# VectorE instead of GpSimd for the low halves of the output weights in the first token block of the first expert layer

## The chip, the cores and the metric

The kernel runs on one core of a Trainium2 chip. The metric is the device time of one execution in microseconds (us), as the median of several executions. One execution was recorded with the hardware profiler; its trace gives every instruction's start and duration. The engines are called as in the profile: PE is TensorE's matrix multiplication and PEld its weight load, DVE is VectorE, ACT is ScalarE, POOL is GpSimd, SP is the engine that issues most of the DMAs.

## The reference, cut to what matters

Three stages follow each other: an attention over 4 x 448 tokens whose heads are mixed before and after the softmax, a dense layer ("first expert layer" here) and a layer of eight experts. The change lies in the dense layer alone, for 1792 tokens:

```python
def _moe_ref(x, w_in, w_out):          # x 1792 x 768
    h = x @ w_in                       # 768 -> 2048
    g = h - np.tanh(h)
    return (g @ w_out).astype(np.float32)   # 2048 -> 768
```

## The kernel before

The dense layer is the function moe1. It cuts the tokens into four blocks of 512, 512, 512 and 256, and the 2048 inner columns into 16 parts of 128; a unit (b, f) is part f of block b. For each unit `first(b, f)` makes the 128 x 512 product h on PE (18 matmuls, line 541), in one of two PSUM banks that alternate (`bank(6)`), and the nonlinearity from it: ACT writes u, d and the two squares (lines 547 to 550), VectorE combines them into g by six instructions (lines 551 to 556), ACT rounds g to ghl's high half (line 558), GpSimd subtracts that from g to get its low half (line 559). Two units later `second(b, f)` multiplies (18 matmuls, line 569): for each of six output chunks high x high, high x low half of g, low half of the weight x high.

The weight halves are whl. `split_wo(b, f)` makes them anew for every block out of wo[f], one unit ahead: ACT rounds to the high half (line 489), and another engine subtracts for the low half, the "rest" (line 490, 128 x 768). In blocks 0 to 2 that engine is GpSimd, in the last block VectorE. whl and ghl have three buffers each.

In block 0 alone, wo[f] itself is made first. `load_wo(f)` loads 64-bit numbers into wor (768 KB, one buffer, line 483), and three VectorE instructions (lines 77, 79 and 81) turn them into float32. As there is one wor, the load of part f+1 starts when line 81 of part f is over. In block 0 VectorE also prepares tables for the routing of the last layer: small instructions on es (8 x 1, lines 436 to 446 and 524), em (line 525), tri (520) and en (532). The router's table en passes through one of the two banks after unit 6 (`prepare_turn`), so that unit 7 gets the bank of unit 6 again, and its first matmul waits until VectorE's line 552 of unit 6 has read it.

Every engine works through its own list in order; the lists are set when the program is built, by a scheduler that works with estimates of durations, so an edit of one instruction can reorder its neighbours.

Of the kernel before, what the change touches and what calls it, by code (L numbers as in the profile page):

```python
# [11 lines left out]
F32 = mybir.dt.float32  # L12
# [28 lines left out]
BLOCKS = [(0, 512), (512, 512), (1024, 512), (1536, 256)]  # L41
# [407 lines left out]
def moe1(tc, ctx, bank, xd, wind, w_out, emb, tau, consts, yg, pos, keep, ids0, chosen):  # L449

    nc = tc.nc
# [13 lines left out]
    wih, wil, wo = {}, {}, {}  # L465
# [21 lines left out]
    def split_wo(b, f):  # L487
        w = p3.tile([128, 2, DM], F32R, tag="whl", name=f"whl_{b}_{f}")
        nc.scalar.copy(w[:, 0], wo[f])  # L489
        (nc.vector if b == len(BLOCKS) - 1 else nc.gpsimd).tensor_tensor(out=w[:, 1], in0=wo[f], in1=w[:, 0].bitcast(F32),  # L490
                                                                         op=ALU.subtract)
        W[b, f] = w

# [272 lines left out]

    units = [(b, f) for b in range(len(BLOCKS)) for f in range(FC)]
    split_wo(0, 0)
    todo = []
    for i, (b, f) in enumerate(units):  # L770
# [6 lines left out]
        if i + 1 < len(units):  # L777
            split_wo(*units[i + 1])
# [386 lines left out]
```

## Time and profile before

| | us |
|---|---|
| time before, median of 3 executions | 1247.13 (1244.72 to 1248.77) |
| profiled execution | 1242.88 |
| its span, first to last instruction | 1241.0 |
| PE busy in the span | 1181.6 (95%) |
| VectorE, ScalarE, GpSimd busy | 852.2, 730.7, 628.2 |
| line 490 on GpSimd, blocks 0 to 2 (48 times) | 89.4, 1863 ns each |

Attention ends at about 462 us; block 0 of the dense layer then fills the time to about 610 us, blocks 1 to 3 that to 949 us, and the expert layer the rest. In the rows below, "idle before" is an engine's idle time just ahead of an instruction, with what ended it behind the arrow. Names without numbers stand for all their buffers.

### The profile page before, as it was taken

How to read it: one execution, taken by the hardware profiler on the slowest of the kernel's cores; microseconds unless marked ns; L12 is line 12 of the kernel's file. 1: busy time of each engine (PE TensorE's matmuls, PEld its weight loads, DVE VectorE, ACT ScalarE, POOL GpSimd, SP SyncE). 2: the span in 40 equal slices, each digit the busy share in tenths (PEclk: the TensorE clock that was granted, in tenths of full speed). 3: DMA queues.
4: the chain of work that ended last, by engine and by line, in shares of the span. 5: the costliest groups of instructions: out<-in, count | busy, mean ns of one | idle time of the engine just before them, and what ended most of it. 6: DMA issues, size and time to landing. Idle time of an engine off the chain costs nothing.

```text
span 1241.0 us, 23758 instructions
## 1 busy us (share of the span) xinstructions
PE 1181.6 (95%) x8624; PEld 834.3 (67%) x8648; DVE 852.2 (69%) x1943; ACT 730.7 (59%) x1499; POOL 628.2 (51%) x546
## 2 busy tenths in 40 slices
PE   8999999999999988999999999999998899999994
PEld 4655665665566654566566666666887678899993
DVE  5887687778877829977767447654788455566661
ACT  6887687678768744444545454554577234555661
POOL 3887688578858753433453335243233233343340
PEclk8999998999999999999999999999999899999998
DMA  6465656556565486223201000010034656678750
GB/s 199 161 215 154 203 186 207 154 190 197 177 197 193 128 246 218 79 100 107 73 1 52 1 26 2 1 51 1 1 130 154 196 192 200 213 253 278 247 201 23
DMA packets 82872, 173.92 MB, mean 140 GB/s; under 512 B 12171, under 2 KB 60171, under 8 KB 82744
## 3 DMA queue, kind: packets, MB, share of 16 engines
q1 hardware_dynamic: 77002, 160.75, 39.9%
q0 software_dynamic: 5472, 11.43, 3.4%
q8 instruction: 70, 1.15, 0.4%
q14 instruction: 58, 0.48, 0.1%
q10 hardware_dynamic: 270, 0.12, 0.1%
HBM read 110.79 MB, written 23.30 MB: 108 GB/s over the span
## 4 chain that ended last, share of the span: by engine, by line
PE 68%; DVE 11%; DMA 9%; issue 4%; ACT 4%; POOL 3%; SPq 1%; ACTq 0%; POOLq 0%; DVEq 0%
PE bank L569 11%; PE bank L541 10%; PE bank L290 9%; PE bank L240 9%; PE bank L948 9%; PE bank L924 9%; PE bank L203 4%; PE bank L305 4%; DMA G<-S 3%; DMA wor<-in_w_out_dram 3%; DVE g L555 1%; DVE wo L81 1%; DVE wo L79 1%; PE bank L977 1%; DVE g L556 1%
## 5 line engine op out<-in xcount | busy, mean ns | idle before, releaser
L569 PE MATMUL bank<-ghl,whl 128*128 128x512 f32 (+1 forms) x1152 | 257.3, 374 | 8.4 <-POOL whl L490 3.0
L569 PEld LDWEIGHTS bank<-ghl,whl 128*128 128x128 f32 x1152 | 198.2, 190 | 49.6 <-POOL whl L490 4.7
L295 POOL TENSOR_TENSOR at<-at 128x480 f16<-128x480 f32 x180 | 176.2, 990 | 48.7 <-ACT at L294 45.7
L240 PE MATMUL bank<-G,wmix 120*120 120x448 f32 x360 | 171.9, 562 | 9.8 <-DMA G<-S 9.0
L290 PE MATMUL bank<-wr,A 120*128 120x120 f32 (+4 forms) x1800 | 171.0, 243 | 3.9 <-DVE wr L272 3.1
L490 POOL TENSOR_TENSOR whl<-wo,whl 128x768 fp32r<-128x768 f32 x48 | 89.4, 1863 | 160.3 <-ACT whl L489 159.8
L244 DVE TENSOR_REDUCE st<-bank 120x1 f32<-120x448 f32 x180 | 111.6, 620 | 52.8 <-PE bank L240 50.5
L250 ACT ACTIVATE A<-bank,st 120x448 f32<-120x448 f32 x180 | 114.9, 639 | 47.4 <-DVE st L244 24.4
L559 POOL TENSOR_TENSOR ghl<-g,ghl 128x512 fp32r<-128x512 f32 (+1 forms) x64 | 78.2, 1221 | 127.3 <-ACT ghl L558 127.3
L294 ACT COPY at<-bank 128x480 f32<-128x480 f32 x180 | 101.6, 566 | 33.1 <-PE bank L290 32.8
L541 PEld LDWEIGHTS <-wih 128*128 128x128 f16 x768 | 71.6, 98 | 72.3 <-issue 13.4
L913 ACT CAST wh_a<-wr_a 128x768 f16<-128x768 f32 x112 | 92.6, 829 | 43.0 <-PE bank L948 33.6
L290 PEld LDWEIGHTS bank<-wr,A 120*128 120x128 f32 (+1 forms) x720 | 91.4, 193 | 36.1 <-issue 20.2
L551 DVE SCALAR_TENSOR_TENSOR g<-bank,u 128x512 f32<-128x512 f32 (+1 forms) x64 | 39.9, 623 | 97.6 <-ACT d L548 97.6
L914 DVE TENSOR_TENSOR wl_a<-wr_a,wh_a 128x768 bf16<-128x768 f32 x84 | 82.4, 983 | 33.6 <-ACT wh_a L913 33.5
L255 POOL TENSOR_TENSOR A<-A 120x448 f16<-120x448 f32 (+1 forms) x90 | 84.4, 938 | 28.2 <-ACT A L250 14.3
L489 ACT CAST whl<-wo 128x768 fp32r<-128x768 f32 x64 | 53.2, 833 | 76.5 <-PE bank L569 56.6
L948 PE MATMUL bank<-rh_a,wl_a 128*128 128x208 f16 (+5 forms) x336 | 86.2, 260 | 0.0
L948 PE MATMUL bank<-rl_a,wh_a 128*128 128x208 bf16 (+5 forms) x336 | 86.2, 260 | 0.0
L924 PE MATMUL bank<-xph_a,wh_a 128*128 128x208 f16 (+5 forms) x336 | 86.2, 259 | 0.0
L948 PE MATMUL bank<-rh_a,wh_a 128*128 128x208 f16 (+5 forms) x336 | 86.2, 259 | 0.0
L541 PE MATMUL bank<-mxh,wih 128*128 128x512 f16 (+1 forms) x384 | 84.1, 354 | 2.1 <-DVE d L552 2.0
(215 smaller groups left out, 2593.1 us busy)
## 6 DMA issues: line engine op xcount, KB each, us to landing
wr_a<-in_w_dram SPq DMA_DIRECT2D x64, 768.0 KB
G<-S SPq DMA_DIRECT2D x176, 210.0 KB
raw_w<-in_w_in_dram SPq DMA_DIRECT2D x32, 384.0 KB
wor<-in_w_out_dram SPq DMA_DIRECT2D x16, 768.0 KB
raw_v<-in_v_dram SPq DMA_DIRECT2D x16, 384.0 KB
yg<-row SPq DMA_DIRECT2D x3, 1540.0 KB
raw_q<-in_q_dram SPq DMA_DIRECT2D x9, 448.0 KB
raw_k<-in_k_dram SPq DMA_DIRECT2D x9, 448.0 KB
```

Of the source, the lines that this page charges most:

```text
L240: nc.tensor.matmul(ps[:r, :S], wmix[:r, :r], g[:r], start=True, stop=True)
L244: latest["dve"] = nc.vector.tensor_reduce(out=st[:r, k:k + 1], in_=ps[:r, :S], axis=AX.X, op=ALU.min)
L250: latest["act"] = nc.scalar.activation(out=a[:r, :S], in_=ps[:r, :S], func=AF.Exp, bias=bias, scale=-1.0, accum_out=st[:r, 4 + k:5 + k])
L290: nc.tensor.matmul(ps[:, jc * r:jc * r + r], x[:r, js], w[:r].rearrange("p (a b) -> p a b", b=10)[:, :, :n], start=(i == 0), stop=(i == le ...
L294: nc.scalar.copy(at32[:, :, t0:t0 + n], v)
L295: nc.gpsimd.tensor_tensor(out=atl[:, :, t0:t0 + n], in0=at32[:, :, t0:t0 + n], in1=ath[:, :, t0:t0 + n], op=ALU.subtract)
L490: (nc.vector if b == len(BLOCKS) - 1 else nc.gpsimd).tensor_tensor(out=w[:, 1], in0=wo[f], in1=w[:, 0].bitcast(F32), op=ALU.subtract)
L541: nc.tensor.matmul(h, u[f][:, c], X[b][v][:, c, :N], start=(i == 0), stop=(i == len(seq) - 1))
L569: nc.tensor.matmul(Y[b][c][:, :N], w[:, u, 128 * c:128 * c + 128], hl[:, v, :N], start=(f == 0 and i == 0), stop=(f == FC - 1 and i == 2))
L913: nc.scalar.copy(wh, raw)
L924: nc.tensor.matmul(h, w[u][:, 128 * c:128 * c + 128], XP[e][v][:, c, :N], start=(i == 0), stop=(i == len(seq) - 1))
L948: nc.tensor.matmul(O[e][c][:, :N], w[u][:, 128 * c:128 * c + 128], r[v], start=(f == 0 and i == 0), stop=(f == MF - 1 and i == 2))
```

## The change

In block 0 too, line 490 is given to VectorE.

```diff
     def split_wo(b, f):
         w = p3.tile([128, 2, DM], F32R, tag="whl", name=f"whl_{b}_{f}")
         nc.scalar.copy(w[:, 0], wo[f])
-        (nc.vector if b == len(BLOCKS) - 1 else nc.gpsimd).tensor_tensor(out=w[:, 1], in0=wo[f], in1=w[:, 0].bitcast(F32),
+        (nc.vector if b in (0, len(BLOCKS) - 1) else nc.gpsimd).tensor_tensor(out=w[:, 1], in0=wo[f], in1=w[:, 0].bitcast(F32),
                                                                          op=ALU.subtract)
```

This takes 16 instructions off GpSimd's list and puts them on VectorE's, and the scheduler places them. The first place is VectorE's list around unit 3, part 2 (in names the first number is the block or wo's part, and g_0_3 is unit 3 of block 0). Before:

```order
L551 SCALAR_TENSOR_TENSOR g_0_3_6737<-bank6_607_6716,u_0_3_6735 128x512
L79 SCALAR_TENSOR_TENSOR wo_2_6581<-wor_2_6579,wo_2_6581 128x768
L552 SCALAR_TENSOR_TENSOR d_0_3_6736<-bank6_607_6716,d_0_3_6736 128x512
L81 SCALAR_TENSOR_TENSOR wo_2_6581<-wor_2_6579,wo_2_6581 128x768
L553 TENSOR_SCALAR u_0_3_6735<-u_0_3_6735 128x512
L554 SCALAR_TENSOR_TENSOR g_0_3_6737<-s1_0_3_6738,g_0_3_6737 128x512
L443 TENSOR_SCALAR es_6514<-es_6514 8x1
L555 SCALAR_TENSOR_TENSOR g_0_3_6737<-s2_0_3_6739,g_0_3_6737 128x512
```

The same place of the changed kernel:

```order
L551 SCALAR_TENSOR_TENSOR g_0_3_6737<-bank6_607_6716,u_0_3_6735 128x512
L79 SCALAR_TENSOR_TENSOR wo_2_6581<-wor_2_6579,wo_2_6581 128x768
L552 SCALAR_TENSOR_TENSOR d_0_3_6736<-bank6_607_6716,d_0_3_6736 128x512
L81 SCALAR_TENSOR_TENSOR wo_2_6581<-wor_2_6579,wo_2_6581 128x768
L553 TENSOR_SCALAR u_0_3_6735<-u_0_3_6735 128x512
L554 SCALAR_TENSOR_TENSOR g_0_3_6737<-s1_0_3_6738,g_0_3_6737 128x512
L438 TENSOR_SCALAR es_6514<-es_6514 8x1
L490 TENSOR_TENSOR whl_0_2_6585<-wo_2_6581,whl_0_2_6585 128x768
L555 SCALAR_TENSOR_TENSOR g_0_3_6737<-s2_0_3_6739,g_0_3_6737 128x512
```

Line 490 has gone in among the steps of g, and the small es instructions lie one group later. For whl_0 to whl_5 it stands so, among the steps of g; whl_5's stands behind line 552 of unit 6. From whl_6 on it stands at another place, directly behind line 81 and ahead of line 551 of the next unit. This is VectorE's list there, unit 9, as a difference:

```order
 L556 COPY_PREDICATED g_8_7112<-u_8_7110,d_8_7111 128x512
 L81 SCALAR_TENSOR_TENSOR wo_7016<-wor_7014,wo_7016 128x768
+L490 TENSOR_TENSOR whl_8_7020<-wo_7016,whl_8_7020 128x768
 L551 SCALAR_TENSOR_TENSOR g_9_7180<-bank_614_7159,u_9_7178 128x512
 L552 SCALAR_TENSOR_TENSOR d_9_7179<-bank_614_7159,d_9_7179 128x512
```

Nothing else moved there. PE, ACT and SP keep their lists but for one neighbour exchanged on PE at unit 3 and one on ACT.

## Rows read from the trace of the kernel before

**Rows 1.** Busy time by stretch (windows): length, each engine's busy us, granted clock, DMA.

```profile
470.00:526.00 56.00, 48.84 (x205) 28.50 (x207) 54.06 (x77) 22.56 (x38) 22.88 (x13) 0.97 0.44 150
526.00:606.00 80.00, 79.74 (x356) 50.55 (x360) 58.27 (x85) 36.95 (x60) 34.18 (x21) 1.00 0.32 109
622.00:948.00 326.00, 321.19 (x1837) 229.12 (x1851) 211.27 (x441) 181.29 (x331) 124.36 (x92) 1.00 0.11 39
```

**Rows 2.** Waits of PE from 470 to 530 us: total, times, longest.

```profile
PE bank L569 <- POOL whl L490: 3.0, 3, 1.2
PE bank L541 <- DVE d L552: 2.0, 1, 2.0
```

**Rows 3.** Timeline about unit 7's start: start, duration, engine, line, instruction.

```profile
517.85 0.67 DVE L552 SCALAR_TENSOR_TENSOR d<-bank,d 128x512 f32<-128x512 f32 x1
...
518.57 1.72 PE L541 MATMUL bank<-mxh,wih 128*128 128x512 f16 x6 [1.98 <-DVE d L552]
...
523.95 4.48 PE L569 MATMUL bank<-ghl,whl 128*128 128x512 f32 x18
```

**Rows 4.** Windows of PE alone there: length, busy, granted clock, DMA.

```profile
518.00:520.00 2.00, 1.43 (x6) 0.91 0.78 200
520.00:522.00 2.00, 1.78 (x5) 0.50 0.47 194
```

**Rows 5.** VectorE from 478 to 518 us, grouped by line: busy us, mean ns.

```profile
L555 DVE SCALAR_TENSOR_TENSOR g<-s,g 128x512 f32<-128x512 f32 x4 | 9.1, 2277 | 0.1
```

**Rows 6.** VectorE from 526 to 598 us, grouped by line.

```profile
L555 DVE SCALAR_TENSOR_TENSOR g<-s,g 128x512 f32<-128x512 f32 x9 | 6.2, 686 | 0.1
```

**Rows 7.** Timeline of units 1 to 5, waits of VectorE and GpSimd on each other.

```profile
477.02 0.56 DVE L77 TENSOR_SCALAR wo<-wor 128x768 uint32<-128x768 uint32 x1 [0.43 <-DMA wor<-in_w_out_dram]
...
479.00 1.28 POOL L559 TENSOR_TENSOR ghl<-g,ghl 128x512 fp32r<-128x512 f32 x1 [3.09 <-ACT ghl L558]
...
479.61 1.48 DVE L81 SCALAR_TENSOR_TENSOR wo<-wor,wo 128x768 uint32<-128x768 uint32 x1
...
482.04 2.27 POOL L490 TENSOR_TENSOR whl<-wo,whl 128x768 fp32r<-128x768 f32 x1 [1.76 <-ACT whl L489]
...
482.66 2.20 DVE L555 SCALAR_TENSOR_TENSOR g<-s,g 128x512 f32<-128x512 f32 x1
...
486.43 1.25 DVE L442 TENSOR_TENSOR es<-es 8x1 f32<-8x1 f32 x1
...
505.35 0.56 DVE L77 TENSOR_SCALAR wo<-wor 128x768 uint32<-128x768 uint32 x1 [0.36 <-DMA wor<-in_w_out_dram]
...
505.94 1.94 DVE L79 SCALAR_TENSOR_TENSOR wo<-wor,wo 128x768 uint32<-128x768 uint32 x1
...
515.38 1.94 DVE L81 SCALAR_TENSOR_TENSOR wo<-wor,wo 128x768 uint32<-128x768 uint32 x1
```

**Rows 8.** Line 490's own instructions: ns shortest, median, longest, first and last start.

```profile
L490 DVE TENSOR_TENSOR whl<-wo,whl x16: 947/958/959, 861.3 to 936.1; 128x768 fp32r<-128x768 f32 x16
```

**Rows 9.** Timeline of one later unit.

```profile
548.01 4.46 PE L569 MATMUL bank<-ghl,whl 128*128 128x512 f32 x18
...
549.12 0.96 DVE L81 SCALAR_TENSOR_TENSOR wo<-wor,wo 128x768 uint32<-128x768 uint32 x1
...
550.04 1.29 POOL L559 TENSOR_TENSOR ghl<-g,ghl 128x512 fp32r<-128x512 f32 x1 [4.84 <-ACT ghl L558]
550.18 0.84 ACT L489 CAST whl<-wo 128x768 fp32r<-128x768 f32 x1 [0.21 <-DVE wo L81]
...
552.10 0.69 DVE L551 SCALAR_TENSOR_TENSOR g<-bank,u 128x512 f32<-128x512 f32 x1 [2.01 <-ACT d L548]
...
554.51 0.56 DVE L77 TENSOR_SCALAR wo<-wor 128x768 uint32<-128x768 uint32 x1 [0.19 <-DMA wor<-in_w_out_dram]
...
556.02 4.46 PE L569 MATMUL bank<-ghl,whl 128*128 128x512 f32 x18
...
557.10 0.95 DVE L81 SCALAR_TENSOR_TENSOR wo<-wor,wo 128x768 uint32<-128x768 uint32 x1
```

## The prediction

> **What bounds the kernel now.** I read the busy time by stretch first. Block 0 falls into two parts. From 526 us on PE is busy for 79.74 of 80 us, and in blocks 1 to 3 for 321.19 of 326; nothing that VectorE or GpSimd does shortens those, unless it makes PE wait. From 470 to 526 us PE is busy for 48.84 of 56 us only, and VectorE for 54.06: here VectorE is the full engine, and the 7.2 us in which PE idles are nearly all that the change can win [rows 1]. The waits of PE in that stretch name two things that touch the change: 3.0 us for line 490 on GpSimd, and one wait of 2.0 us for line 552 on VectorE [rows 2]. The timeline shows the second: line 552 of unit 6 ends at 518.52 us, and only then can unit 7's first matmul start, after 1.98 us of idleness, in the one bank that two units in a row share [rows 3]. From there PE runs without a gap. So the end of block 0, and with it the end of the kernel, moves one for one with the moment at which VectorE is through line 552 of unit 6. What PE waits for before that moment only makes it wait longer there: removing the 3.0 us alone buys nothing. That idle time also costs clock: the granted clock is 0.91 and then 0.50 (the lower of the two levels, 1.2 GHz) in the two windows behind it [rows 4], and unit 7's 18 matmuls take from 518.57 to 523.95 us [rows 3], 5.4 us, where a whole later unit of 36 takes 8.01 us, of which the second 18 take 4.46 [rows 9]: some 1.8 us lost.
>
> **The change, part by part.** The sum is made on VectorE's list, from line 81 of part 1, which ends at 481.09 us [rows 7], to line 552 of unit 6, which ends at 518.52.
>
> First, what is removed. GpSimd's line 490 runs while VectorE stands at line 555. In the first case GpSimd's instruction ends at 482.04 + 2.27 = 484.31 us, and line 555, begun at 482.66, ends at 484.86, 0.55 us later [rows 7]: it did its work once GpSimd was through. Line 555 has two inputs in SBUF, one of them g, the other a square from ACT. From 478 to 518 us the four of line 555 take 2277 ns each [rows 5], the nine later ones 686 ns [rows 6]: 4 x 1.59 = 6.4 us come back when GpSimd has no line 490.
>
> The Trainium skill says the same of the cause (SBUF — State Buffer, "Who interferes with whom"): a VectorE instruction with two SBUF inputs and a GpSimd instruction that reads SBUF exclude each other, and whichever was first holds the port for its whole length. The trace agrees (0.55 us after 484.31).
>
> Second, what is added. Between the two points VectorE gets whl_1 to whl_4; whl_0 comes before, whl_5 behind line 552 of unit 6. The trace has line 490 on VectorE in the last block, same shape, 958 ns [rows 8]: 4 x 0.96 = 3.8 us. whl_0 costs nothing: VectorE then waits for the load of part 1 until 477.02 us (0.43 us idle) [rows 7]; without that cover it would be 0.96.
>
> Third, GpSimd's line 559 (1.28 us) stays, and holds VectorE in the same way: line 81 at 479.61 us takes 1.48 instead of 0.95 us [rows 7, 9]. In the stretch of the sum it costs VectorE now at most 1.25 us at 486.43, and 0.99 us each at 505.94 and 515.38 (1.94 against 0.95): 3.2 us [rows 7]. In the new order lines 77 and 79 of the next part stand right behind line 556 in every unit, and line 559 starts about when line 79 wants the port, so I take four full waits: 4 x 0.99 = 4.0, that is 0.8 us more. Bounds: none more; or five waits, 1.8 us more.
>
> Fourth, the start and the load. In the new order line 81 of part 1 stands ahead of line 551 of unit 2 and behind line 556 of unit 1, so it ends before line 559 gets going, and the stretch begins 0.5 us earlier (its 1.48 us becomes 0.95). The load of a part starts when line 81 of the part before ends; line 77 waited 0.36 us for one at 505.35 [rows 7]. VectorE arrives sooner for parts 4 and 5, so I take 0.2 us more of that, with bounds of 0 and 0.4.
>
> Sum: 6.4 - 3.8 - 0.8 + 0.5 - 0.2 = 2.1 us less. Best by the bounds: 6.4 - 3.8 + 0.5 = 3.1 less. Worst: five line 490 (4.8), 1.8, 0.4 and no earlier start: 6.4 - 7.0 = 0.6 us more.
>
> Fifth, the later units (whl_6 to whl_15). VectorE has room, 58.27 us busy of 80 [rows 1], but its chain is tight: line 81 recurs after 7.98 us (549.12 to 557.10), PE's line 569 after 8.01 [rows 9]. Line 490 stands ahead of line 551 of the next unit, which idles 2.01 us for ACT. Line 81 ends at 550.08; ACT's cast ends at 551.02; GpSimd's line 559 holds the port to 551.33; line 490, if held till then, ends at about 552.2, where line 551 began at 552.10 [rows 9]. So it is hidden in that idle time but for 0.1 us, and that by the 0.19 us for which line 77 waited for its load anyway. I take nothing. Without this cover each unit's chain would grow by 0.96 - 0.19 = 0.77 us. Blocks 1 to 3 and GpSimd's remaining work are untouched.
>
> The profiled execution took 1242.88 us, so 1240.8 for such a one. It is 1.8 us below the fastest of the three executions timed; their median is 1247.13, and the same 2.1 us off it gives 1245.0.
>
> **The rivals.** (a) The clock stays up: if PE's wait before unit 7 gets short, the 1.8 us go too, 3.9 us in all, 1243.2. For it: VectorE is earlier by 2.1 us, more than the wait of 1.98. Against: PE comes earlier too, since the 3.0 us for line 490 fall away, so the wait rather grows, to about 1.98 + 3.0 - 2.1 = 2.9 us, and then the low clock stays.
>
> (b) Slower: VectorE, full as it is, just gets longer. If the waits of line 555 were not GpSimd's line 490 but would come at another instruction of the same stretch, nothing of the 6.4 us comes back: 3.8 + 0.8 + 0.2 - 0.5 = 4.3 us more, 1251.4. It decides from the point at which less than 4.3 / 4 = 1.1 of the 1.59 us per unit returns. For it: 54.06 of 56 us, and line 559 that is free to move into every gap. Against: the 0.55 us above.
>
> The Trainium skill speaks for this side (Perfetto Trace Analysis, "Optimizing Scalar/DVE Operations"): work that is moved between GpSimd and VectorE might not gain, as they share a read port. By that alone the time would not fall. The trace bears the sharing out, but the same subtraction takes 2.27 us on GpSimd there, its own waiting included [rows 7], and 0.96 on VectorE [rows 8].
>
> (c) The later chain: line 490 fails to fit into the idle time, and VectorE's chain grows by 0.77 us in each of ten units, 7.7 us. PE would feel only what goes beyond its lead: ghl is finished at 551.33 us for a line 569 at 556.02, 4.7 us [rows 9]. So 3.0 us come through, and with the 2.1 won it is 0.9 more, 1248.0. Against: the sums above, which leave 0.1 us.
>
> **How the numbers follow.** 0.3% is 3.7 us, about what a measurement can tell from no change. The forecast, with its own range from 3.1 less to 0.6 more (1244.0 to 1247.7), has a chance of 0.58 and lies within 0.3%. (a) has 0.20 and is just faster; (b) 0.10 and slower; (c) 0.12 and the same. So faster 0.20, the same 0.70, slower 0.10. The executions before spread from 1.6 above to 2.4 below their median, so the range goes from (a) less 2.4 to (c) plus 1.6: 1240.8 to 1249.6. It leaves out (b) and the far edges of the others.
>
> **What would show it.** Right: line 555 from 478 to 518 us at about 0.69 us; line 490 on VectorE at 0.96 us, with or without a wait for line 559; no wait of PE for line 490 on GpSimd; line 552 of unit 6 about 2 us earlier and PE's wait for it 2 to 3 us; line 569 still every 8.01 us later on. Wrong: the clock at full level behind unit 7's start (a); waits of VectorE behind line 559 that add up to more than 6 us (b); line 569 at more than 8.1 us in the later units (c).

## The result, and the profile after

The changed kernel took 1234.30 us as the median of 6 executions (1233.18 to 1238.42), against 1247.34 of 6 of the kernel before: 0.9913 of the time, with a 95% interval of 0.989 to 0.9935. The forecast was 1245.0 and its range ended at 1240.8. Two more sets of executions gave 0.9929 (0.9905 to 0.9952) and 0.994 (0.9917 to 0.9963), so the first set lay at the low end. Over all sets, 25 executions of after have a mean span of 1235.7 us and 134 of before one of 1244.1: 8.4 us less, four times the 2.1 that were forecast. The profiled execution of after took 1235.33 us with a span of 1233.6. One execution of a later experiment, late_units, took 1976 us at a granted clock of 0.556, and is left out of all means.

Busy time by stretch, after (length; busy us of PE, PEld, DVE, ACT, POOL; granted clock; DMA):

```profile
470.00:526.00 56.00, 51.47 (x228) 31.39 (x227) 51.06 (x88) 23.48 (x38) 9.71 (x7) 1.00 0.42 146
526.00:606.00 80.00, 79.64 (x371) 49.84 (x373) 66.53 (x96) 39.10 (x65) 17.32 (x12) 1.00 0.30 99
```

VectorE's busy time fell from 54.06 to 51.06 us in the first stretch although it has more instructions [rows 1]: what it lost is time spent holding still. VectorE grouped by line from 478 to 518 us (busy, mean ns | idle before), after:

```profile
L79 DVE SCALAR_TENSOR_TENSOR wo<-wor,wo 128x768 uint32<-128x768 uint32 x5 | 7.7, 1536 | 0.1
...
L490 DVE TENSOR_TENSOR whl<-wo,whl 128x768 fp32r<-128x768 f32 x5 | 4.7, 948 | 0.0
L555 DVE SCALAR_TENSOR_TENSOR g<-s,g 128x512 f32<-128x512 f32 x5 | 3.4, 689 | 0.1
```

Line 555 went from 2277 to 689 ns [rows 5], line 490 costs 948 ns, and line 79 now waits behind line 559. The stretch of the sum ends at 512.91 us, so one of the five of lines 79, 490 and 555 lies behind it. One small es instruction waits behind line 559 too, after:

```profile
490.93 1.29 POOL L559 TENSOR_TENSOR ghl<-g,ghl 128x512 fp32r<-128x512 f32 x1 [6.32 <-ACT ghl L558]
491.11 1.12 DVE L444 TENSOR_TENSOR es<-es 8x1 f32<-8x1 f32 x1
```

PE's waits from 470 to 530 us, after:

```profile
PE bank L541 <- DVE d L552: 3.4, 2, 3.2
PE bank L569 <- POOL ghl L559: 0.7, 1, 0.7
PE bank L569 <- DVE whl L490: 0.3, 1, 0.3
```

The 3.0 us of waits for GpSimd's line 490 are gone and the wait for line 552 has grown from 2.0 to 3.2 us [rows 2]. The timeline there, after:

```profile
508.78 1.93 DVE L79 SCALAR_TENSOR_TENSOR wo<-wor,wo 128x768 uint32<-128x768 uint32 x1
...
512.23 0.68 DVE L552 SCALAR_TENSOR_TENSOR d<-bank,d 128x512 f32<-128x512 f32 x1
512.96 1.46 PE L541 MATMUL bank<-mxh,wih 128*128 128x512 f16 x6 [3.16 <-DVE d L552]
...
516.65 4.46 PE L569 MATMUL bank<-ghl,whl 128*128 128x512 f32 x18
```

The clock behind the wait, in windows of PE, after:

```profile
516.00:518.00 2.00, 2.00 (x11) 1.00 0.02 4
518.00:520.00 2.00, 2.00 (x10) 1.00 0.00 0
```

In this execution the clock stayed at the higher level in spite of 3.16 us of waiting, and unit 7's 18 matmuls took 3.69 us (512.96 to 516.65), where they took 5.38 before [rows 3, 4]. One later unit, after:

```profile
548.71 4.46 PE L569 MATMUL bank<-ghl,whl 128*128 128x512 f32 x18
...
550.25 0.95 DVE L81 SCALAR_TENSOR_TENSOR wo<-wor,wo 128x768 uint32<-128x768 uint32 x1
551.15 1.30 POOL L559 TENSOR_TENSOR ghl<-g,ghl 128x512 fp32r<-128x512 f32 x1 [6.59 <-ACT ghl L558]
551.24 0.84 ACT L489 CAST whl<-wo 128x768 fp32r<-128x768 f32 x1 [0.16 <-DVE wo L81]
552.10 1.17 DVE L490 TENSOR_TENSOR whl<-wo,whl 128x768 fp32r<-128x768 f32 x1 [0.90 <-ACT whl L489]
553.19 0.68 DVE L551 SCALAR_TENSOR_TENSOR g<-bank,u 128x512 f32<-128x512 f32 x1
...
556.72 4.46 PE L569 MATMUL bank<-ghl,whl 128*128 128x512 f32 x18
557.05 0.56 DVE L77 TENSOR_SCALAR wo<-wor 128x768 uint32<-128x768 uint32 x1 [1.65 <-DMA wor<-in_w_out_dram]
```

Line 490 stands in VectorE's idle time, 0.90 us of it ahead of line 490 and 1.65 ahead of line 77, and line 569 recurs after 8.01 us as before [rows 9].

### The profile page after: what moved, and what is told of

The parts are those of the page before. It is cut to its first block, busy times and chain, and to the rows that moved or that the text cites. A ratio compares the mean times of both kernels' runs of the same rounds, so it can differ in the third digit from the quotient of the medians.

```text
span 1233.6 us, 23781 instructions
## 1 busy us (share of the span) xinstructions
PE 1180.5 (96%) x8648; PEld 832.8 (68%) x8648; DVE 857.3 (70%) x1959; ACT 729.8 (59%) x1499; POOL 597.0 (48%) x530
## 4 chain that ended last, share of the span: by engine, by line
PE 68%; DVE 11%; DMA 10%; issue 4%; ACT 3%; POOL 3%; SPq 0%; POOLq 0%; ACTq 0%; DVEq 0%
PE bank L569 12%; PE bank L541 10%; PE bank L290 9%; PE bank L240 9%; PE bank L948 8%; PE bank L924 8%; PE bank L203 5%; PE bank L305 4%; DMA G<-S 4%; DMA wor<-in_w_out_dram 3%; DVE wo L81 1%; DVE wo L79 1%; PE bank L977 1%; DVE g L555 1%; DMA yg<-row 1%
## 5 line engine op out<-in xcount | busy, mean ns | idle before, releaser
L490 POOL TENSOR_TENSOR whl<-wo,whl 128x768 fp32r<-128x768 f32 x32 | 59.2, 1850 | 136.5 <-ACT whl L489 136.4
```

## How work and clock are told apart

Every execution comes with its span and its mean granted clock. I split a span into span x clock ("work") and the rest ("clock"). This holds only as far as PE sets the pace: a fall of the clock (a stretch at its lower level, 0.50 in the rows) where PE waits for VectorE anyway is counted as clock, though it costs no time. Within the 134 executions of before the span does rise by 0.98 us for each 0.001 of clock that is missing, where the split takes 1.24. Means, with standard errors:

| kernel(s) | executions | span | clock | work | lost to the clock |
|---|---|---|---|---|---|
| before | 134 | 1244.1 ±0.3 | 0.9809 | 1220.3 ±0.2 | 23.8 ±0.3 |
| after | 25 | 1235.7 ±0.7 | 0.9838 | 1215.7 ±0.4 | 20.0 ±0.7 |
| early_units | 12 | 1239.8 ±0.7 | 0.9818 | 1217.2 ±0.4 | 22.5 ±0.6 |
| late_units, late_again, late_pad | 35 | 1240.8 ±0.6 | 0.9831 | 1219.8 ±0.3 | 21.0 ±0.6 |
| placebo_v, placebo_g, block2_late | 36 | 1244.0 ±0.5 | 0.9803 | 1219.5 ±0.4 | 24.5 ±0.6 |

By this split after won about 4.6 us of work and 3.8 us of clock. The second number is loose: the first two sets of after lost 18.3 and 18.4 us to the clock, the third, of 11 executions, 22.0 ±1.0.

That the split can fail shows in block 0. Three of the five traces of before (both placebos and block2_late) have a fall of the clock between 490 and 501 us, this one in placebo_v:

```profile
497.00:500.00 3.00, 3.00 (x8) 0.50 0.02 6
```

From the first line 541 to unit 7 these three take 73.3 to 73.6 us, the two without that fall 73.2 and 73.6.

The traces give a second split, by place: starts of the same PE instruction. The dense layer begins with the first line 541; line 606 first runs at the border of blocks 0 and 1; line 948 begins the expert stage. Us between them, mean of the traces (of before: before, before2, the placebos and block2_late, which are alike up to 750 us; late: late_units, late_again, late_pad):

| from, to | before (5) | late (3) | after (3) |
|---|---|---|---|
| start, first 541 | 446.1 (442.3 to 450.5) | 446.8 | 445.7 |
| first 541, unit 7 | 73.5 (73.2 to 73.6) | 73.3 (72.9 to 74.2) | 71.1 (70.8 to 71.3) |
| unit 7, first 606 | 102.8 (101.9 to 103.5) | 100.4 (100.3 to 100.6) | 100.8 (99.7 to 102.6) |
| first 606, first 948 | 335.8 | 336.2 | 335.3 |
| first 948, end | 284.5 (283.5 to 284.9) | 283.7 | 283.2 |

## The experiments

**Which units?** early_units has the change for whl_0 to whl_5 alone, late_units for whl_6 to whl_15 alone; before2 and after2 are the two kernels again.

```diff
-        (nc.vector if b == len(BLOCKS) - 1 else nc.gpsimd).tensor_tensor(
+        (nc.vector if b == len(BLOCKS) - 1 or (b == 0 and f < 6) else nc.gpsimd).tensor_tensor(    # early_units; late_units: f >= 6
```

> The kernel before, unchanged, run against itself. If the profiled execution of before is typical, its stages have the same lengths here: the attention up to the dense layer's first matmul 445.0 us, from there to the first matmul of unit 7 73.6 us, PE waits about 2 us for line 552 there and unit 7's 18 matmuls take 5.4 us at half clock. Rival (chance): clock falls in the attention or behind unit 7's wait come and go from execution to execution; then these stretches differ by 2 to 3 us between the two traces. Ratio 1.000, with an interval that says how small a difference can be told.

> The changed kernel once more, to see which of its trace's differences recur. Theory A (port waits and clock): from the dense layer's first matmul to unit 7's first matmul 70.8 us, 2.8 less than before; unit 7 at full clock, 3.7 us. Theory B (chance outside the dense layer): the 2.85 us that the attention took less in the first trace of the changed kernel, and the 2.4 us of the expert layer, are not seen again, and the ratio comes closer to 0.997. If the ratio stays at 0.991 although the traces differ by some 2 to 5 us only, something is missing from both.

> Line 490 on VectorE for whl_0 to whl_5 of block 0 only; whl_6 to whl_15 stay on GpSimd. VectorE's list up to unit 6 is that of the changed kernel. Theory A: all of the gain is there, so the ratio to before is that of the changed kernel (0.991) within 0.001. Rival C (the later units count, by GpSimd's port time from 526 us on): less than half of the gain, 0.996 or more.

> Line 490 on VectorE for whl_6 to whl_15 of block 0 only; whl_0 to whl_5 stay on GpSimd, VectorE's list up to unit 6 is that of before. Theory A: PE is full from unit 7 on, so nothing: 1.000 within 0.001, with line 569 every 8.01 us. Rival C: more than half of the gain, 0.995 or less.

Measured: before2 1.000 (0.998 to 1.002), after2 0.9929, early_units 0.9962 (0.9945 to 0.9979), late_units 0.9962 (0.9944 to 0.9979); 1241.95 and 1241.21 us against 1245.92. Each half gives half, where the expectations had all of it in one. By the table the early half is work (3.1 us less) and the late half is clock; for the late half the section on the prediction shows another reading.

**Is it any edit?** The placebos put one small memset per unit into block 2, on VectorE or on GpSimd. late_again repeats late_units; late_pad gives GpSimd a memset for each line 490 it lost; block2_late moves ten line 490 of block 2 instead.

```diff
+        if b == 2:
+            nc.vector.memset(idle[:, 0:1], 0.0)      # placebo_v; placebo_g: nc.gpsimd
...
+        if b == 0 and f > 5:
+            nc.gpsimd.memset(idle[:, 0:1], 0.0)      # late_pad
```

> The kernel before plus 16 tiny memsets (128 x 1, of a tile nobody reads) on VectorE in block 2 of the dense layer; line 490 as before. It asks whether a kernel's median moves by several us for no reason in its stages. If the half of the gain that the late units gave is such luck of a program as a whole (where clock falls and DMA waits happen to lie), this may move by 3 to 5 us either way, 0.996 or 1.004. If the gains have causes in the changed instructions, 1.000 within 0.002.

> The same with the 16 tiny memsets on GpSimd instead of VectorE. Luck of a program: 3 to 5 us either way, and not by the same amount as with the memsets on VectorE. Causes in the changed instructions: 1.000 within 0.002.

> The kernel of late_units once more. If its higher clock belongs to the kernel: mean clock 0.984 again, against 0.981 of the kernel before beside it, and about 1241 us. If it was chance of one set of executions: 0.981 and 1246 us.

> The later units alone (whl_6 to whl_15 on VectorE), with a GpSimd memset of two numbers per partition in the place of each line 490 taken from GpSimd, so that GpSimd's list has as many instructions as before. What is looked at is the mean granted clock of the executions (before 0.981, late_units 0.984) and the span times that clock (before 1220, late_units 1219.9). Theory A (GpSimd's own work in the later units keeps the clock low): as late_units, clock 0.984, about 1241 us. Theory B (the length of GpSimd's list and where its code lies decides): as before, clock 0.981, about 1246 us.

> Before, with line 490 of the later units of block 2 (f from 6 on) on VectorE instead of GpSimd: ten instructions fewer on GpSimd, as in late_units, at another place. Block 2 was bound by TensorE before, so nothing is won there by itself. Theory A (the later units of block 0 are what matters): clock 0.981, about 1246 us. Theory B (ten instructions fewer on GpSimd, wherever): clock 0.984, about 1241 us.

Measured: placebos 1.001 (0.9991 to 1.0029) and 0.9994 (0.9971 to 1.0016), block2_late 1.0014 (0.9997 to 1.0031): an edit as such does nothing. late_again 0.9975 (0.9954 to 0.9996), clock 0.9828; late_pad 0.9981 (0.996 to 1.0002), clock 0.9824. So the late half's first value was high; over its three kernels it loses 2.8 us less to the clock than before (21.0 ±0.6 against 23.8 ±0.3), late_pad by itself 2.0 us less. That the length of GpSimd's list decides is not borne out by block2_late; between late_pad and late_again the intervals overlap.

The traces also show what is chance. In attention, 250 us ahead of the change, a fall of the clock costs 5.1 us in some executions. Windows of PE there, in before, after, late_again and block2_late:

```profile
210.00:215.00 5.00, 5.00 (x19) 0.50 0.56 180
```

```profile
210.00:215.00 5.00, 5.00 (x40) 1.00 0.80 238
```

```profile
215.00:220.00 5.00, 5.00 (x14) 0.50 0.54 168
```

```profile
210.00:215.00 5.00, 5.00 (x40) 1.00 0.64 211
```

It is there in four of the five traces of before and in two of the three of after, so the clean step of attention in the first trace of after (110.3 us, where before takes 115.1) was chance and no effect of the change. The attention as a whole makes 2.9 of the 7.4 us between the two profiled spans (442.1 against 445.0).

**GpSimd's work itself.** no_rest leaves line 490 out in block 0 (the matmul reads the high half of the weight instead), late_none only for units 6 to 15; pool_twice does the later ones twice on GpSimd.

```diff
+        if b > 0:                                    # no_rest; late_none: if b > 0 or f < 6
...
-                nc.tensor.matmul(Y[b][c][:, :N], w[:, u, 128 * c:128 * c + 128], hl[:, v, :N],
+                nc.tensor.matmul(Y[b][c][:, :N], w[:, u if b else 0, 128 * c:128 * c + 128], hl[:, v, :N],
...
+        for _ in range(2 if b == 0 and f > 5 else 1):    # pool_twice, around line 490
```

> Line 490 is left out in block 0 altogether (the matmuls that read the rest read the high half instead), on neither engine. Theory A: VectorE loses the 6.4 us of waits behind line 490 and gets nothing in exchange, so line 552 of unit 6 comes 3 to 4 us earlier than in the changed kernel, and the time is 0.003 below the changed kernel's ratio. Rival C (the gain comes from GpSimd's port time in the later units): the same time as the changed kernel.

> Before, with line 490 left out for the later units of block 0 (f from 6 on); the matrix multiplication reads the high half of the weight in its place there. Neither GpSimd nor VectorE has the work. If taking it off GpSimd is what raises the clock: as late_units, mean clock about 0.984, span times clock 1220, some 1241 us. If it is chance, or VectorE's being busier: clock 0.981, 1246 us, as before.

> Before, with line 490 done twice on GpSimd for the later units of block 0 (f from 6 on), the second time with the same result: ten instructions more on GpSimd where late_units has ten fewer. Theory A by dose: the clock falls further, to about 0.977, and the time rises to about 1250 us. If only the step from one to none counts, or chance: 0.981 and 1246 us.

Measured: no_rest 1235.62 us, 0.9921 (0.989 to 0.9953), work 1213.6 ±0.9. That is 2.1 ±1.0 us less work than after; unit 7 starts 1.4 us earlier than in after (69.7 us behind the first line 541, against 71.1), where 3 to 4 were expected. late_none took 1349.13 us, because its expert stage ran 390 us instead of 284: its trace has matrix multiplications on tiles of a second round (xph_b, from 1248.5 us on) that no other trace has. In the code that round is for tokens beyond those that an expert's first round holds, so the halves left out have changed the routing, and its total says nothing here. Up to the first line 606 its one trace can be read: unit 7 to line 606 took 102.5 us, as before, with a fall of the clock at the border. So the late gain is not shown to come from GpSimd's rest alone. pool_twice took 1259.27 us, 1.0121 (1.0101 to 1.0141), at an unchanged clock of 0.980. PE's waits from 520 to 620 us, and GpSimd by line from 526 to 606, in pool_twice (its lines lie one further down: 491 is 490, 570 is 569):

```profile
PE bank L570 <- POOL whl L491: 12.7, 9, 4.0
```

```profile
L491 POOL TENSOR_TENSOR whl<-wo,whl 128x768 fp32r<-128x768 f32 x18 | 33.1, 1842 | 4.3 <-ACT whl L489 3.6
L560 POOL TENSOR_TENSOR ghl<-g,ghl 128x512 fp32r<-128x512 f32 x8 | 10.2, 1274 | 33.2 <-ACT ghl L559 33.2
```

The second pass, 1.84 us each, makes whl late and PE waits for it: a new bound, so the dose tells nothing of the clock. It does show that the later units had less than 1.84 us of room on GpSimd.

**The shared bank.** after_bank and before_bank take one more turn of the banks behind the router's table, so that unit 7 no longer needs unit 6's bank.

```diff
             nc.tensor.matmul(...)      # prepare_turn() has been issued
+            bank(6)
```

> The changed kernel, with one more turn of the two banks after en, so that unit 7 gets en's bank and not unit 6's: its first matmul waits for VectorE's copy of en (line 532, over at 510.84 us in the changed kernel's trace) and not for line 552 (512.91). Theory A (block 0 ends one for one with that wait): PE's wait before unit 7 falls from 3.2 to about 1.2 us, no clock fall behind it, and the time is 2 us below the changed kernel's, 3 with the clock falls that it has in some executions. Rival: the wait comes back at another unit, since VectorE is no earlier, and nothing is gained.

> Before, with the extra bank turn behind the router's table, so that unit 7's first matrix multiplication no longer waits for line 552 of unit 6. By the prediction's reading VectorE's time to line 552 of unit 6 sets the start of unit 7 in before; without the shared bank TensorE runs on until the next thing VectorE or GpSimd is late with. If the shared bank alone costs what after_bank showed against after (2 us): the two steps to unit 7's first matrix multiplication take 71 instead of 73.4 us, no clock fall behind it, 1243 us. If in before GpSimd's line 490, of which the whl halves are waited for, is the bound there: the wait comes back at line 569, 73 us, and 1246 as before.

Measured: after_bank 1237.66 us, 0.9947 (0.9925 to 0.997), not the 2 us below after that were expected; first 541 to unit 7 takes 68.0 us, 3.1 less than in after, but block 0 as a whole (first 541 to first 606) 170.9 against 171.9, with a fall of the clock at the border. before_bank 1244.66 us, 0.9986 (0.9969 to 1.0003); unit 7's wait for line 552 is gone there too, but block 0 as a whole takes 177.05 us, as long as before (176.3). PE's waits from 515 to 620 us, before_bank:

```profile
PE bank L598 <- DVE yt L577: 2.0, 2, 1.2
PE bank L598 <- ACT yt L579: 1.4, 1, 1.4
```

PE waited there 3.4 us in all, and the clock fell behind it. VectorE starts the last of the copies that PE waits for (line 577) 170.3 us behind the first line 541, where the traces of before have 169.8 to 170.2. So "one for one with line 552 of unit 6" holds for the start of unit 7, not for the end of the kernel: with that wait gone PE waits for VectorE at the border.

**The border.** edge moves line 490 of the first four units of block 1 as well, edge_bank has the extra turn beside it, all_vector moves every line 490.

```diff
-        (nc.vector if b in (0, len(BLOCKS) - 1) else nc.gpsimd).tensor_tensor(
+        (nc.vector if b in (0, len(BLOCKS) - 1) or b == 1 and f < 4 else nc.gpsimd).tensor_tensor(    # all_vector: nc.vector
```

> After, with line 490 of the first four units of block 1 on VectorE too. At the border of blocks 0 and 1 VectorE's line 556 stands behind GpSimd's line 490 (1.85 us where it takes 0.75) and TensorE waits 1.7 us for yt behind it. If that wait is line 490's doing, line 556 takes 0.75 us there, the wait falls below 0.7 us, the step from line 598 to line 606 takes 6.2 to 7.2 us (after: 10.5 and 6.2), no clock fall behind it, and the time is 1 to 3 us less than of after: 1233 to 1236. If VectorE, having four more instructions, is late itself: as after, about 1237.

> After with both: line 490 of the first four units of block 1 on VectorE, and the extra bank turn by which unit 7 doesn't share unit 6's bank. If each gain stands by itself: 1232 to 1236 us, span times clock about 1214 (after_bank 1215.3). If the waits only come back at the next place: 1237, as after_bank.

> Line 490 on VectorE in every block; beside edge this moves the other 28 of blocks 1 and 2, where TensorE is busy without a gap. By the busy times these give nothing within the blocks: as edge, 1233 to 1236 us. If taking line 490 off GpSimd raises the clock wherever it stands, the mean clock rises above after's 0.985 and the time falls below 1232.

> After once more, with twelve executions beside those of before, to split its gain: the span times the mean granted clock 1216 to 1217 against 1220 (3 to 4 us by the work), and a clock of 0.985 against 0.981 (some 5 us by the clock); 1235 to 1237 us. If the clock's share was chance of the first two sets: clock 0.981 to 0.982, 1241 us.

Measured: edge 1235.45 us, 0.9903 (0.987 to 0.9937); edge_bank 1237.34, 0.9923 (0.9894 to 0.9952); all_vector 1239.07, 0.9922 (0.9892 to 0.9952); after_3, 1238.86, 0.994, work 1215.0, clock 0.9822. None can be told from after; the clock of all_vector (0.983) is not above that of after, so nothing shows that taking line 490 off GpSimd raises it wherever it stands. The timeline of the border in before:

```profile
612.86 0.68 DVE L577 COPY yt<-bank 128x512 f32<-128x512 f32 x1
612.90 1.84 POOL L490 TENSOR_TENSOR whl<-wo,whl 128x768 fp32r<-128x768 f32 x1 [3.11 <-ACT whl L489]
613.46 1.85 DVE L556 COPY_PREDICATED g<-u,d 128x512 f32<-128x512 int32 x1
...
615.22 0.67 DVE L577 COPY yt<-bank 128x512 f32<-128x512 f32 x1
...
615.94 0.42 PE L598 MATMUL bank<-yt,en 128*32 128x128 f32 x8 [1.70 <-DVE yt L577]
```

and in edge:

```profile
606.94 0.69 DVE L577 COPY yt<-bank 128x512 f32<-128x512 f32 x1
607.54 0.95 DVE L490 TENSOR_TENSOR whl<-wo,whl 128x768 fp32r<-128x768 f32 x1
...
608.41 0.72 DVE L556 COPY_PREDICATED g<-u,d 128x512 f32<-128x512 int32 x1
609.02 0.68 DVE L577 COPY yt<-bank 128x512 f32<-128x512 f32 x1
...
609.76 0.42 PE L598 MATMUL bank<-yt,en 128*32 128x128 f32 x8 [1.43 <-DVE yt L577]
```

GpSimd's line 490 held line 556 for 1.1 us, as expected. But on VectorE line 490 stands between the same two copies with 0.95 us of its own: the second copy starts 2.08 us after the first instead of 2.36, and PE's wait falls only from 1.70 to 1.43. The expectation (below 0.7) overlooked that the moved instruction lands in the same gap.

## Why the prediction was wrong

**The sum was right.** Line 555 at 689 ns (0.69 forecast), line 490 at 948 (958), PE's wait before unit 7 at 3.16 (2.9), no wait for GpSimd's line 490. The waits behind line 559 in the stretch of the sum were four, as forecast: three of line 79 and one of line 444, 3.9 us in all against 4.0. The earlier start was smaller than forecast: in the first trace of after line 81 of part 1 did take 0.95 us, but the load of part 1 came later, and line 81 ends 36.0 us behind the first line 541 where it ended at 36.1, so 0.1 us earlier and not 0.5. From the first line 541 to unit 7 the traces of after need 2.4 us less (71.1 against 73.5), against 2.1 forecast. early_units alone takes 70.2.

**The first step that failed** is "From there PE runs without a gap. So the end of block 0, and with it the end of the kernel, moves one for one". There is a gap at the border of blocks 0 and 1, where PE waits for VectorE's copies, line 577, 2.0 us in the trace of before and 1.70 of it for the last copy. The windows of rows 1 end at 606 and begin again at 622 us, and leave the place out. So what counts is VectorE's list up to that last copy and not up to line 552 of unit 6. Us from the first line 541, means of the traces:

| kernel (traces) | line 552 of unit 6 | of unit 8 | last line 577 | line 606 |
|---|---|---|---|---|
| before (5) | 72.7 | 92.1 | 170.1 (169.8 to 170.2) | 176.3 (175.5 to 176.9) |
| late (3) | 72.6 | 91.3 | 168.4 (167.8 to 169.3) | 173.7 (173.1 to 174.6) |
| early_units (1) | 69.5 | 88.0 | 165.5 | 172.4 |
| after (3) | 70.4 | 88.2 | 166.0 (165.5 to 166.5) | 171.9 (170.9 to 173.4) |

From the last line 577 to line 606 it takes 5.3 us in the traces without a fall of the clock behind it, 6.7 to 6.9 in those with one. VectorE's gain (from unrounded means) is 2.4 us at unit 6, where the sum ended, 3.9 at unit 8 and 4.0 at the border; line 606 comes 4.4 us earlier, in place of 2.1. before_bank bears this out: there unit 7 has no wait, and the last copy still starts after 170.3 us. The further 1.5 us between units 6 and 8 come from two sides: early_units has 0.8 of them, the late kernels 0.7. For the early side one sees GpSimd's line 490 of part 5 hold VectorE just behind the end of the sum, at line 553, which takes 0.42 us in after. Before:

```profile
518.32 1.82 POOL L490 TENSOR_TENSOR whl<-wo,whl 128x768 fp32r<-128x768 f32 x1 [1.81 <-ACT whl L489]
518.44 1.98 DVE L553 TENSOR_SCALAR u<-u 128x512 int32<-128x512 f32 x1
```

VectorE's last copy gains 1.7 us more than unit 7's start, and in two of the three traces of after PE lost 1.7 us behind unit 7; so PE's wait at the border shrinks, from 2.9 us in the traces of before to 1.0 in those of after, on average. The last copy and PE's wait for it in after2:

```profile
612.49 0.67 DVE L577 COPY yt<-bank 128x512 f32<-128x512 f32 x1
...
613.22 0.43 PE L598 MATMUL bank<-yt,en 128*32 128x128 f32 x8 [0.36 <-DVE yt L577]
```

What PE waits there also depends on what it lost at unit 7. Read from the traces (wait ahead of unit 7; the step from its first line 541 to line 569, 3.7 us or, with a fall of the clock, 5.2 to 5.4; wait at the border; the step from line 598 to line 606, which takes 10 us or more with a fall):

| traces | wait, unit 7 | step | wait, border | step |
|---|---|---|---|---|
| before, placebo_g | 2.0 | 5.4 | 2.0 | 8.1 |
| before2, placebo_v, block2_late | 0.8 to 1.5 | 3.7 | 3.3 to 3.6 | 10.7 to 10.9 |
| before_bank | 0.0 | 3.7 | 3.4 | 10.7 |
| late_units, late_again, late_pad | 1.5 to 1.7 | 3.7 | 2.1 to 2.2 | 8.2 to 8.5 |
| early_units | 3.2 | 3.7 | 2.2 | 10.0 |
| after | 3.2 | 3.7 | 2.6 | 10.5 |
| after2, after_3 | 3.1, 3.2 | 5.4 | 0.4, 0.0 | 6.2, 6.0 |
| edge | 3.1 | 3.7 | 1.7 | 7.8 |
| after_bank | 1.1 | 3.7 | 3.0 | 10.8 |
| edge_bank | 1.0 | 3.7 | 2.0 | 8.3 |
| all_vector | 3.3 | 5.2 | 0.0 | 5.7 |
| no_rest | 2.2 | 3.7 | 1.3 | 7.2 |
| late_none | 1.7 | 3.7 | 2.5 | 10.4 |

The two traces of before with the fall behind unit 7 reach line 606 after 175.5 us, the three with the fall at the border after 176.6 to 176.9: the 1.7 us lost at unit 7 were waited for at the border anyway.

**The second** is "I take nothing" for the later units. Line 569 does recur after 8.01 us, but the late kernels have VectorE's last copy 1.7 us earlier than before, and 1.5 when counted from unit 7, with no overlap of the traces (95.0 to 95.2 us behind unit 7, against 96.5 to 96.8). Some 0.7 us arise by unit 8, and 0.7 at the border, where the line 490 of the last part is gone from GpSimd. In before three of line 490 follow each other there, the last part's and two of block 1, and hold line 554; in late_units two hold line 555. Before:

```profile
600.09 5.63 POOL L490 TENSOR_TENSOR whl<-wo,whl 128x768 fp32r<-128x768 f32 x3 [1.81 <-ACT whl L489]
...
603.92 2.35 DVE L554 SCALAR_TENSOR_TENSOR g<-s,g 128x512 f32<-128x512 f32 x1
```

and in late_units:

```profile
600.31 2.04 POOL L490 TENSOR_TENSOR whl<-wo,whl 128x768 fp32r<-128x768 f32 x1 [1.04 <-ACT whl L489]
...
600.65 2.24 DVE L555 SCALAR_TENSOR_TENSOR g<-s,g 128x512 f32<-128x512 f32 x1
```

Block 0 is 2.5 us shorter in the late kernels, of their 3.3 us of span (1244.1 to 1240.8): 1.7 by the last copy and 0.9 by the fall at the border, which three of the five traces of before have and none of the three late ones. The split by the mean clock calls 2.8 of the 3.3 us clock, since the late traces have no fall at all in block 0; but the falls of before ahead of unit 7 and right behind it cost nothing at the end of block 0. Why the late kernels have no fall at the border is not shown. No rule of the wait's length comes out of the table: behind 2.1 to 2.2 us at the border the clock stayed up in the late kernels and fell in early_units, and late_none, with 1.7 and 2.5, had the fall. No run set the waits by themselves.

**The third** is the place of the clock in the sum. Rival (a) counted 1.8 us behind unit 7 as the clock's share, in one place, tied to the length of one wait. The runs show that in before such a fall behind unit 7 costs nothing at the end of block 0, and that there are falls in attention, at the border and in the expert stage as well; some come and go between executions of one kernel: behind unit 7 in two of the three traces of after, each time after a wait of 3.1 to 3.2 us, and not in the third, after 3.16. By the split before lost 23.8 us to the clock altogether, after 20.0. The Trainium skill (TensorE: Matmul & The Clock Gate, "The HAM clock gate (the 'warmup' mystery)") says that the same kernel shows a different number of slow matmuls from run to run; these traces agree (unit 7's 18 matmuls took 3.69 us in one trace of after and 5.38 in two). The range was built from the spread of three executions and from (a) alone, and so ended at 1240.8.

**What stays open.** Of the 8.4 us, 4.4 lie between the first line 541 and line 606 (2.4 and 2.0). Another 0.6 lie in blocks 1 to 3 and 1.3 in the expert stage (283.2 against 284.5), where no instruction was changed; the late kernels have 0.8 of it, early_units none (285.6). The cause was not found. The remaining 2.1 are not seen in the three traces of after, but for 0.4 in attention; whether attention's falls, which come and go, are rarer in after was not settled.

**The rivals.** (b) did not happen: 1.59 of the 1.59 us per unit came back. (c) did not: the later chain stayed at 8.01 us. (a), the clock staying up behind unit 7, is seen in one of the three traces of after, though its condition, a short wait, was not met there (3.16 us), and the clock fell at the border instead.

## What to carry to other kernels

When an instruction is moved off GpSimd, count the VectorE instructions that stood still behind it, those with one SBUF input too (line 553 here); that difference against its own length on VectorE was here a good forecast up to the place where the sum ended. Carry the sum on to the last place where PE waits for VectorE, and leave no gap between the windows that are read: here the gain grew from 2.4 to 4.0 us behind the end of the sum. And when TensorE waits for a microsecond or two in several places, read the granted clock of many executions before and after, and give the forecast a range of that size: by the split the clock's share was here nearly as large as the work's.

## What was not expected of the hardware

The granted clock fell to its lower level (1.2 GHz) behind a wait of PE of 2.0 us in one kernel, and stayed up after one of 3.16 in another. One such fall lengthened unit 7's 18 matmuls by 1.7 us (5.38 for 3.69), yet block 0 of before ended no later for it; with falls a step of attention took 115.1 us in place of 110.3. Over an execution the split makes this 20 to 24 us, 1.6 to 1.9% of the span, and most of the spread between executions of one kernel: before's lay between 1238.9 and 1253.0 us.

Line 553, with one SBUF input, was held by GpSimd's line 490 as line 555 with two was: 1.98 us against 0.42.
